# RWKV-6 attention and MLP on one core: the D product is scaled in its PSUM bank, and the order is dealt anew

## The chip, the core and the metric

The kernel runs on one core of one Trainium2 chip. Its engines run side by side, each through its own queue in order: TensorE (PE: matmuls; PEld: its weight loads), VectorE (DVE), ScalarE (ACT), GpSimd (POOL) and SyncE (SP), which issues most DMAs. Matmuls write PSUM, which has eight banks; the other engines read it from there. The metric is device time in microseconds, the median of several runs.

## The reference

A linear attention with a decaying state, then a layer norm and a two-layer MLP with a residual. Batch 4, 8 heads, 768 steps, head size 48, so 384 features; the hidden layer has 1536.

```python
for t in range(S):
    kt, vt, rt, wt = (k[:, :, t], v[:, :, t], r[:, :, t], w[:, :, t])
    cur = np.einsum('bhd,bhe->bhde', u[None] * kt, vt)
    y[:, :, t] = np.einsum('bhd,bhde->bhe', rt, state + cur)
    state = wt[:, :, :, None] * state + np.einsum('bhd,bhe->bhde', kt, vt)
x = np.ascontiguousarray(attn_out.transpose(0, 2, 1, 3)).reshape(B, S, H * D)
mu = np.mean(x, axis=-1, keepdims=True)
var = np.mean((x - mu) ** 2, axis=-1, keepdims=True)
xn = (x - mu) / np.sqrt(var + 1e-06) * g_ln
ch = np.maximum(xn @ w_ch1, 0.0) @ w_ch2
return (x + ch).astype(np.float32)
```

## The kernel before

**Rounds.** The work is cut into eight rounds: four batches, two halves of 384 steps each. A round's `front` does the attention. It transposes `w`, `k` and `r` on TensorE (`w_ps`, `k_ps`, `r_ps`) and builds the products of steps within blocks of 64 in six levels. `quads` issues a level's matmuls (output `a`, 48 rows deep, packed four at a time into quarters of the array), `grow` multiplies `k` and `r` by decay products on VectorE before the next level, and `keep` collects the results. Then come `states` (tiled matmuls of `k` and `v`), and `outputs` (more tiled matmuls into `a`). The matmuls of these three use quarters of TensorE's array and are called tiled here; all others use the whole array. `back` normalizes and runs the MLP.

**The MLP in three parts.** For rounds 1 to 7 (`THREE = 1`) the first product is not done in full fp32. The input is split into a high part H, a low part L and a difference D = L - H/4096; the weights into a high part, the rest times 4096, and the difference of these two. With E12 = 1/4096, the product is (1 + E12)(L product + H product) + D product, with each part in the format fp32r. For a chunk `f` of 128 hidden features (twelve to a round, 84 in all) `mlp` plans:

- `stream`: SyncE fetches the D weights, `d`.
- `go_d` (L1466): three matmuls of D into a bank `hd_ps`. The trace has one record for each.
- `copy` (L1474): ScalarE copies that bank to `h` in SBUF, which frees the bank.
- `go` (L1479): three matmuls of L (`wl`) and three of H (`wh`) into a second bank `h_ps`.
- `add` (L1491): VectorE makes `h = (1 + E12) * h_ps + h`.
- rounds 1 to 4: `relu` (L1497) on ScalarE, in place in SBUF, then the second product in plain fp32 (`o`, three groups of output rows, four times three hidden chunks each; two records a matmul).
- rounds 5 to 7 (`LAST = NR - 3`): `thirds` (L1332). ScalarE makes the relu'd high part H (`high`), VectorE a low part (`low`) and a difference (`diff`), and nine matmuls bring a chunk into the output, D into one bank, L and H into another. After the last chunk VectorE adds the D bank to `x` (`add`), then (1 + E12) times the other (`rest`), and SyncE stores.

Round 0 does the first product in plain fp32 (`first_product`, `h_ps<-xf,w`).

**What sets the order.** No order is written out. Each step is given to `plan.add` with an engine, a cost, what it reads and writes, and a priority; `Plan.order` deals all of them out, engine by engine, simulating the time by those costs. `SHIFTS` (L90) moves priorities, `WAIT` says how much later an engine may start a step of better priority, `STAY` what a change between tiled and whole-array matmuls counts for TensorE, `PATIENCE` how long GpSimd may hold off beside VectorE. A step marked `EITHER` goes to VectorE or GpSimd, whichever the plan finds free. Where TensorE would stand idle in the first 90 us, the plan puts fillers (`idle`), matmuls on zeros.

**Buffers.** `HOMES` gives each kind of tile its number of places: twelve for `h`. PSUM has two double banks `a` for the tiled work (in rounds 5 to 7 they hold two of the three output row groups) and four banks `b` for everything else; the third output row group takes two of the four in rounds 5 to 7 (`o_2P`, `o_2D`). A place comes free when the plan has seen its last reader.

Helper `InOrder` issues every instruction, so nearly all rows of the profile carry its line, L50, and are told apart by the names of their tiles.

```python
plan.add("ACT", 0.45, copy, r=[ps_d], w=[h_], pri=EVICT)
plan.add("DVE", 0.53, add, r=[ps], w=[h_], pri=EVICT)
```

Of the kernel before, what the change touches and what calls it, by code (L numbers as in the profile page):

```python
# [10 lines left out]
F32 = mybir.dt.float32  # L11
# [5 lines left out]
AF = mybir.ActivationFunctionType  # L17
ALU = mybir.AluOpType
# [48 lines left out]
class Plan:  # L67
# [11 lines left out]

    HOP, MARGIN, FILLED, PATIENCE, STAY = 0.1, 0.05, 60.0, 15.1983, 20.0356
    BEFORE, PIECE, FETCH, CROWD = 66, 256, 3.72835, 300
    WAITS = 1.006
    DRAIN = {True: 0.1, False: 0.12}
    WAIT = {"PE": 0.0403625, "ACT": 0.191784, "DVE": 0.109619, "POOL": 0.0526016, "SP": 0.0742572}

    SHIFTS = {  # L90
        -280: 9, -217: 13, -40: 14, -19: 28, -6: 19.5, 0: 8, 1: -20.5, 5: -18, 6: -131.5, 11:
        -21, 16: -8, 18: -18.5, 38: -9.5, 42: 5, 48: -51.5, 52: -22.5, 58: -28, 61: -5, 64: -42,
        67: -35, 88: 4.5, 98: -23, 120: -1, 130: -51, 131: 13, 136: -3, 162: 3.5, 170: -9, 172:
        -17, 174: 11, 182: 43, 184: -6, 204: 2, 205: 9, 206: 40.5, 209: 2, 212: -3, 247: 46,
        262: -4.5, 289: 34, 301: 0.5, 319: -15, 407: 3.5, 411: 9.5, 413: 11, 415: -8, 417: 57,
        423: 52, 441: 13, 448: 6, 451: 114.5, 452: -3.5, 453: 12, 455: 15, 465: -2.5, 480: -32,
        489: 49, 493: 18.5, 499: 9, 502: 10.5,
    }

    def __init__(self, homes, dynamic):  # L100
# [176 lines left out]
def kernel(  # L277
# [147 lines left out]
    def at(rnd, stage):  # L425
        return 40 * rnd + stage
# [661 lines left out]
    def x_parts(rnd, kc):  # L1088
        return [
            tile_(tag, name, [P, 1 if tag == "rest" else 2, RN], F32R)[:, i]  # L1090
            for tag, name, i in x_places(rnd, kc)
        ]
# [238 lines left out]

    def thirds(rnd, f):  # L1332

        x_, h_, (g, c) = f"x{rnd}", f"h{rnd}_{f}", divmod(f, KC + 1)
        b, f0 = rounds[rnd]
        H_, L_, D_ = (f"h{n}{rnd}_{f}" for n in "HLD")
        pri = at(rnd, FILL) + 2 * f + 3
# [1 line left out]
        def out_tiles(i):  # L1339
            if i < 2:  # L1340
                t = tile_("a", f"o{rnd}_{i}", None)
                return t[:, 0, 0:RN], t[:, 1, 0:RN]
            return [tile_("b", f"o{rnd}_{i}{n}", [P, RN]) for n in "PD"]
# [15 lines left out]
                in1=tiles[L_].bitcast(F32), op0=ALU.mult, op1=ALU.add,  # L1359
            )  # L1360

        plan.add("ACT", 0.53, high, r=[h_], w=[H_], new=[("h", H_)], pri=at(rnd, 30))
        plan.add("DVE", 0.56, low, r=[h_, H_], w=[L_], new=[("h", L_)], pri=at(rnd, 30), port=True)
        plan.add("DVE", 0.5, diff, r=[H_, L_], w=[D_], new=[("h", D_)], pri=at(rnd, 30), port=True)
        first, last = f == 0, f == FC - 1
        whole = x_of(rnd)
        for i in range(TT):
            o = f"o{rnd}_{i}"
            names = [o] if i < 2 else [o + "P", o + "D"]

            def go_d(i=i):
                PE.matmul(
                    out_tiles(i)[1], tiles[D_][:, ts(i, P)], tiles[f"w2d{f}"], start=first, stop=last
                )

            def go(i=i):
                to = out_tiles(i)[0]
                PE.matmul(
                    to, tiles[L_][:, ts(i, P)], tiles[f"w2l{g}"][:, c], start=first, stop=False
                )  # L1380
                PE.matmul(
                    to, tiles[H_][:, ts(i, P)], tiles[f"w2h{g}"][:, c], start=False, stop=last
                )

            def both(i=i):
                go_d(i)
                go(i)

            def add(i=i):
                x = tiles[x_][:, i]  # L1390
                DVE.tensor_tensor(
                    out=x, in0=out_tiles(i)[1].rearrange("p (h d) -> p h d", d=D), in1=x, op=ALU.add
                )

            def rest(i=i):
                x = tiles[x_][:, i]
                DVE.scalar_tensor_tensor(
                    out=x, in0=out_tiles(i)[0].rearrange("p (h d) -> p h d", d=D),
                    scalar=1.0 + E12, in1=x, op0=ALU.mult, op1=ALU.add,
                )  # L1400

            def store(i=i):
                SP.dma_start(
                    out=out[b, ds(f0 * RN + i * P, P), :].rearrange("t (h d) -> t h d", d=D),
                    in_=tiles[x_][:, i],
                )

            keys = [o + n if i == 2 else (o, n) for n in "PD"]
            need = [H_, L_, D_, f"w2d{f}", (f"w2h{g}", c), (f"w2l{g}", c)]
            if first:  # L1410
                need += x_of(NR - 1)
            if last and rnd == NR - 1:

                plan.add("PE", 0.18, go_d, count=2, r=need, w=keys[1:], pri=pri - 100, lat=0.17)
                plan.add("PE", 0.36, go, count=4, r=need, w=keys[:1], pri=pri, lat=0.17)
            else:
                plan.add(
                    "PE", 0.525, both, count=6, r=need, w=keys,
                    new=[("a" if i < 2 else "b", n) for n in names] if first else [],
                    pri=pri, lat=0.17,  # L1420
                )
            if last:
                plan.add("DVE", 0.53, add, r=[keys[1]] + whole, w=[(x_, "sum", i)], pri=EVICT)
                plan.add("DVE", 0.53, rest, r=[keys[0], (x_, "sum", i)], w=[(x_, "out", i)], pri=EVICT)
                plan.add("SP", 0.36, store, r=[(x_, "out", i)], pri=EVICT, lat=2.0, size=0.65)
# [27 lines left out]
    def mlp(rnd):  # L1453
# [3 lines left out]
        for f in range(FC):  # L1457
            pri = at(rnd, FILL) + 2 * f * (rnd >= LAST)
            h_, ps, g, cols = f"h{rnd}_{f}", f"h_ps{rnd}_{f}", f // G, ts(f % G, P)
            tag = "h" if rnd < LAST + (f < KC) else ("rk", "vo", "vo")[f % 3]  # L1460
            if rnd < THREE:
                continue
            ps_d, d_ = f"hd_ps{rnd}_{f}", f"d{rnd}_{f}"
            stream(rnd, f)

            def go_d(ps_d=ps_d, d_=d_):  # L1466
                t = tile_("b", ps_d, [P, RN])
                for kc in range(KC):
                    PE.matmul(
                        t, tiles[d_][:, kc], x_parts(rnd, kc)[2],  # L1470
                        start=kc == 0, stop=kc == KC - 1,
                    )

            def copy(h_=h_, ps_d=ps_d, tag=tag):  # L1474
                if tag != "h":
                    tiles[h_] = homes.tile([P, NH * ROW], F32, tag=f"{tag}{plan.place[h_]}", name=h_)[:, 0:RN]
                ACT.copy(out=tile_(tag, h_, [P, RN]), in_=tiles[ps_d])

            def go(ps=ps, g=g, cols=cols):  # L1479
                t = tile_("b", ps, [P, RN])  # L1480
                for kc in range(KC):
                    PE.matmul(
                        t, tiles[f"wl{g}"][:, kc, cols], x_parts(rnd, kc)[1], start=kc == 0, stop=False
                    )
                for kc in range(KC):
                    PE.matmul(
                        t, tiles[f"wh{g}"][:, kc, cols], x_parts(rnd, kc)[0],
                        start=False, stop=kc == KC - 1,
                    )

            def add(h_=h_, ps=ps):  # L1491
                DVE.scalar_tensor_tensor(
                    out=tiles[h_], in0=tiles[ps], scalar=1.0 + E12, in1=tiles[h_],
                    op0=ALU.mult, op1=ALU.add,
                )

            def relu(h_=h_):  # L1497
                ACT.activation(out=tiles[h_], in_=tiles[h_], func=AF.Relu)

            plan.add(  # L1500
                "PE", 0.53, go_d, count=6, r=[d_] + [x_keys(rnd, kc)[2] for kc in range(KC)], w=[ps_d, ps_d + "t"],
                new=[("b", ps_d), (tag, h_)], pri=pri,
                lat=0.17,
            )
            plan.add("ACT", 0.45, copy, r=[ps_d], w=[h_], pri=EVICT)
            plan.add(
                "PE", 1.11 if rnd < LAST else 1.05, go, count=12,
                r=[(f"wl{g}", kc) for kc in range(KC)] + [(f"wh{g}", kc) for kc in range(KC)]
                + [key for kc in range(KC) for key in x_keys(rnd, kc)[:2]]
                + [ps_d if rnd < LAST else ps_d + "t"],  # L1510
                w=[ps], new=[("b", ps)], pri=pri - 0.1, lat=0.17,
            )
            plan.add("DVE", 0.53, add, r=[ps], w=[h_], pri=EVICT)
            if rnd >= LAST:
                thirds(rnd, f)
                continue
            plan.add("ACT", 0.53, relu, w=[h_], pri=at(rnd, 30))
        if rnd >= LAST:
            return
        for i in range(TT):  # L1520
# [178 lines left out]
```

## Time and profile before

| | |
|---|---|
| runs | 526.66, 522.78, 523.22 us; median 523.22 |
| profiled execution, first to last instruction | 521.6 us |
| between it and the median of the runs | 1.6 us |
| first and last matmul | 0.99 us, 517.5 us |
| granted TensorE clock | 0.999 on average |
| bytes moved | 55.84 MB, mean 107 GB/s |

How to read it: the page gives for each engine its busy time, share of the span and number of instructions. A group of instructions is written out<-in with its shapes, the number of instructions, then busy us, mean ns of one, then the idle time of the engine just before them and what ended it. A timeline row is: start in us, time in us, engine, line, operation, out<-in, shapes, number of instructions, and in brackets the idle time before it and what ended that. Matmuls overlap, so the time of a row is longer than the step to the next row's start; a "duration" of 338 ns goes with a start every 176. `issue` means that the engine waited for nothing that the profile shows.

### The profile page before, as it was taken

Reading aid. Unit: us, or ns where it says so; the run is one execution under the profiler, and the core shown is the slowest. Engines: PE = TensorE matmul, PEld = TensorE weight load, DVE = VectorE, ACT = ScalarE, POOL = GpSimd, SP = SyncE. Lnnn points to the kernel's source line nnn. Section 1 sums busy time; section 2 is a strip of 40 time slices with the busy share of each in tenths; the row PEclk is TensorE's granted clock in tenths of the full one; section 3 lists DMA queues with packets and bytes.
Section 4 is the critical chain, followed back from the end, with each engine's and each line's share of the span. In section 5 each row is a group of like instructions: output and inputs, shape, how many; then the busy total and the mean of one; then the engine's idle time right before and its main releaser. Section 6 shows DMA issues by size and latency. Waiting matters only on the chain.

```text
span 521.6 us, 20645 instructions
## 1 busy us (share of the span) xinstructions
PE 514.1 (99%) x8998; PEld 434.4 (83%) x8998; DVE 397.5 (76%) x844; ACT 270.8 (52%) x603; POOL 72.2 (14%) x106
## 2 busy tenths in 40 slices
PE   9999999999999999999999999999999999999996
PEld 6788888767998777989866897589767999999996
DVE  5888999889999898998985773168757867665555
ACT  3798888874375362664630984027373534332321
POOL 7212301221141031122200220003000000000000
PEclk9999999999999999999999999999999999999999
DMA  9966885278635716756420415022012422222201
GB/s 216 257 173 164 192 219 153 76 176 208 164 63 111 179 30 124 163 105 121 126 52 18 98 55 140 17 87 58 1 33 65 134 62 90 77 61 91 77 0 47
DMA packets 122362, 55.84 MB, mean 107 GB/s; under 512 B 93984, under 2 KB 119200, under 8 KB 122272
## 3 DMA queue, kind: packets, MB, share of 16 engines
q1 hardware_dynamic: 119152, 53.54, 40.9%
q10 hardware_dynamic: 3120, 0.98, 1.0%
q8 instruction: 71, 1.16, 0.9%
q14 instruction: 19, 0.16, 0.1%
HBM read 45.05 MB, written 7.10 MB: 100 GB/s over the span
## 4 chain that ended last, share of the span: by engine, by line
PE 97%; DVE 1%; ACT 1%; issue 1%; DVEq 0%
PE a L50 26%; PE o L50 22%; PE h_ps L50 22%; PE hd_ps L50 9%; PE w_ps L50 3%; PE k_ps L50 3%; PE r_ps L50 3%; PE idle L50 3%; PE o_2P L50 2%; PE kn_ps L50 2%; PE xT_ps L50 1%; PE o_2D L50 1%; DVE xhl L50 0%; DVE x L50 0%; DVE xd L50 0%
## 5 line engine op out<-in xcount | busy, mean ns | idle before, releaser
L50 PE MATMUL o<-ffn,h 128*128 128x384 f32 x360 | 124.9, 491 | 0.0
L50 PEld LDWEIGHTS o<-ffn,h 128*128 128x128 f32 x360 | 65.5, 190 | 37.1
L50 ACT COPY h<-hd_ps 128x384 f32<-128x384 f32 x84 | 40.3, 481 | 72.6 <-PE hd_ps L50 70.9
L50 DVE SCALAR_TENSOR_TENSOR h<-h_ps,h 128x384 f32<-128x384 f32 x84 | 46.7, 556 | 39.9 <-PE h_ps L50 37.8
L50 PEld LDWEIGHTS a<-r,k 48*63 48x63 f32 (+5 forms) x4608 | 63.4, 126 | 15.9 <-issue 6.6
L50 PE MATMUL a<-r,k 48*63 48x32 f32 (+5 forms) x4608 | 69.6, 212 | 1.0 <-issue 0.9
L50 PE MATMUL h_ps<-xhl,wl 128*128 128x384 f32 x252 | 59.8, 345 | 0.0
L50 PE MATMUL h_ps<-xhl,wh 128*128 128x384 f32 x252 | 57.7, 337 | 0.0
L50 PE MATMUL hd_ps<-xd,d 128*128 128x384 f32 x252 | 55.5, 346 | 0.1
L50 DVE TENSOR_TENSOR k<-k,tot 112x768 f32<-112x768 f32 (+1 forms) x50 | 40.2, 805 | 18.8 <-PE a L50 18.5
L50 PEld LDWEIGHTS hd_ps<-xd,d 128*128 128x128 f32 x252 | 44.1, 188 | 2.0 <-issue 0.7
L50 PEld LDWEIGHTS h_ps<-xhl,wh 128*128 128x128 f32 x252 | 45.2, 188 | 0.0
L50 PEld LDWEIGHTS h_ps<-xhl,wl 128*128 128x128 f32 x252 | 44.2, 188 | 1.1
L50 DVE COPY_PREDICATED A<-mask,a 128x768 f32<-128x768 int8 (+2 forms) x36 | 39.5, 1097 | 1.1 <-PE a L50 1.1
L50 DVE TENSOR_TENSOR r<-r,tot 112x768 f32<-112x768 f32 (+1 forms) x50 | 39.6, 791 | 0.0
L50 ACT ACTIVATE hH<-h 128x384 fp32r<-128x384 f32 x36 | 18.5, 524 | 37.9 <-DVE h L50 30.0
L50 ACT ACTIVATE h<-h 128x384 f32<-128x384 f32 x48 | 25.2, 526 | 20.8 <-DVE h L50 20.6
L50 ACT COPY A<-a 32x384 f32<-32x384 f32 (+2 forms) x36 | 15.6, 433 | 36.5 <-PE a L50 36.1
L50 DVE SCALAR_TENSOR_TENSOR hL<-h,hH 128x384 fp32r<-128x384 f32 x36 | 20.0, 555 | 10.8 <-ACT hH L50 10.5
L50 POOL TENSOR_TENSOR rk<-nat,nat 128x576 f32<-128x576 f32 (+1 forms) x13 | 17.8, 1368 | 74.9 <-PE a L50 19.7
L50 PE MATMUL h_ps<-xf,w 128*128 128x128 f32 (+1 forms) x144 | 26.3, 332 | 0.0
L50 ACT COPY r<-r_ps 112x384 f32<-112x384 f32 (+1 forms) x31 | 14.2, 493 | 23.2 <-PE r_ps L50 23.1
(119 smaller groups left out, 1007.7 us busy)
## 6 DMA issues: line engine op xcount, KB each, us to landing
d<-w1d SPq DMA_DIRECT2D x84, 192.0 KB, 2.9
raw<-in_moe_w_ch_dram SPq DMA_DIRECT2D x24, 384.0 KB, 4.3
v<-in_v_dram SPq DMA_DIRECT2D x48, 96.0 KB, 3.3
out_dram<-x SPq DMA_DIRECT2D x24, 192.0 KB, 2.0
nat<-in_w_dram SPq DMA_DIRECT2D x36, 96.0 KB, 3.4
nat<-in_k_dram SPq DMA_DIRECT2D x36, 96.0 KB, 3.1
nat<-in_r_dram SPq DMA_DIRECT2D x36, 96.0 KB, 3.2
w1d<-w1diff SPq DMA_DIRECT2D x12, 192.0 KB, 4.0
```

Source lines behind the costliest of these rows:

```text
L50: ins = self.tc.keep_in_program_order(f(*args, **kw))
```

## The change

The D product stays in its bank. ScalarE multiplies the bank in place by 1/(1 + E12) (`shrink`), and the L and H matmuls accumulate on it instead of starting a bank of their own. The bank then holds the first product divided by (1 + E12). VectorE's `add` and the SBUF copy are gone. In rounds 1 to 4 the relu reads the bank, multiplies by (1 + E12) and writes `h`. In rounds 5 to 7 `high` and `low` read the bank itself, without the factor, so the final `add` and `rest` of `thirds` carry one factor of (1 + E12) more. The place for `h` (or for H, L and D) is taken when the D product starts.

The constants of the plan and all of `SHIFTS` are replaced, so the whole order of all engines differs, and so does what `EITHER` gives to GpSimd: its products fall from 70 to 44. The matmuls are the same in kind and number, but for the fillers.

```diff
-    HOP, MARGIN, FILLED, PATIENCE, STAY = 0.1, 0.05, 60.0, 15.1983, 20.0356
+    HOP, MARGIN, FILLED, PATIENCE, STAY = 0.1, 0.05, 60.0, 36.9760452, 44.9511633
-    WAIT = {"PE": 0.0403625, "ACT": 0.191784, "DVE": 0.109619, "POOL": 0.0526016, "SP": 0.0742572}
+    WAIT = {"PE": 0, "ACT": 0.1862803, "DVE": 0.1548472, "POOL": 0.157666, "SP": 0.7767392}
     SHIFTS = {
-        -280: 9, -217: 13, -40: 14, -19: 28, -6: 19.5, 0: 8, 1: -20.5, 5: -18, 6: -131.5, 11:
+        -472: 60.5, -360: -211.5, -38: -20.5, -32: -113.5, -31: -113.5, -29: -113.5, -22: -111.5,
...
     def thirds(rnd, f):
-        x_, h_, (g, c) = f"x{rnd}", f"h{rnd}_{f}", divmod(f, KC + 1)
+        x_, h_, (g, c) = f"x{rnd}", f"h_ps{rnd}_{f}", divmod(f, KC + 1)
...
             def add(i=i):
-                DVE.tensor_tensor(
-                    out=x, in0=out_tiles(i)[1].rearrange("p (h d) -> p h d", d=D), in1=x, op=ALU.add
+                DVE.scalar_tensor_tensor(
+                    out=x, in0=out_tiles(i)[1].rearrange("p (h d) -> p h d", d=D),
+                    scalar=1.0 + E12, in1=x, op0=ALU.mult, op1=ALU.add,
                 )
...
             def rest(i=i):
...
-                    scalar=1.0 + E12, in1=x, op0=ALU.mult, op1=ALU.add,
+                    scalar=(1.0 + E12) ** 2, in1=x, op0=ALU.mult, op1=ALU.add,
...
-            def go_d(ps_d=ps_d, d_=d_):
-                t = tile_("b", ps_d, [P, RN])
+            def go_d(ps=ps, d_=d_):
+                t = tile_("b", ps, [P, RN])
...
-            def copy(h_=h_, ps_d=ps_d, tag=tag):
...
-                ACT.copy(out=tile_(tag, h_, [P, RN]), in_=tiles[ps_d])
+            def shrink(ps=ps):
+                ACT.activation(out=tiles[ps], in_=tiles[ps], func=AF.Copy, scale=1 / (1 + E12))
...
             def go(ps=ps, g=g, cols=cols):
-                t = tile_("b", ps, [P, RN])
-                    PE.matmul(
-                        t, tiles[f"wl{g}"][:, kc, cols], x_parts(rnd, kc)[1], start=kc == 0, stop=False
-                    )
...
+                for n, nm in ((1, "l"), (0, "h")):
+                    for kc in range(KC):
+                        PE.matmul(
+                            tiles[ps], tiles[f"w{nm}{g}"][:, kc, cols], x_parts(rnd, kc)[n],
+                            start=False, stop=(n, kc) == (0, KC - 1), skip_group_check=True,
+                        )
-            def add(h_=h_, ps=ps):
-                DVE.scalar_tensor_tensor(
-                    out=tiles[h_], in0=tiles[ps], scalar=1.0 + E12, in1=tiles[h_],
-                    op0=ALU.mult, op1=ALU.add,
-                )
-            def relu(h_=h_):
-                ACT.activation(out=tiles[h_], in_=tiles[h_], func=AF.Relu)
+            def relu(h_=h_, ps=ps):
+                ACT.activation(
+                    out=tile_("h", h_, [P, RN]), in_=tiles[ps], func=AF.Relu, scale=1 + E12
+                )
```

The three `plan.add` of the chunk (D matmuls, `shrink`, L and H matmuls) write the same bank, one after another; before, the D bank and the L and H bank were two tiles; the plan put L and H after D, but they waited for no ScalarE.

## The prediction

> **What bounds the kernel now.** I read the page's first part, its slices and its chain of waits, then the busy time by stretch, then TensorE's timeline, then the groups that the change touches.
>
> ```profile
> span 521.6 us, 20645 instructions
> PE 514.1 (99%) x8998; PEld 434.4 (83%) x8998; DVE 397.5 (76%) x844; ACT 270.8 (52%) x603; POOL 72.2 (14%) x106
> ...
> PE 97%; DVE 1%; ACT 1%; issue 1%; DVEq 0%
> ```
>
> The chain is TensorE's own queue for 97% of its length. Where time could still be lost is read from the stretches (us from the start; length; busy time of each engine, TensorE first):
>
> ```profile
> 0.00:60.00 60.00, 57.06 (x1291) 46.81 (x1292) 48.18 (x131) 44.97 (x104) 20.70 (x53) 1.00 0.82 198
> 60.00:130.00 70.00, 69.92 (x1324) 54.37 (x1323) 64.37 (x130) 52.60 (x123) 10.53 (x12) 1.00 0.68 170
> 130.00:380.00 250.00, 249.57 (x5372) 204.14 (x5371) 193.43 (x393) 120.98 (x269) 39.92 (x41) 1.00 0.38 90
> 400.00:521.00 121.00, 117.53 (x755) 115.36 (x753) 77.47 (x152) 40.64 (x84) 1.02 (x1) 1.00 0.23 69
> ```
>
> From 60 us on TensorE has no gaps worth the name (0.08 of 70 us, 0.43 of 250), at a granted clock of 1.00. A busy TensorE can still be slow, so I take its starts, one matmul to the next, at the middle of each kind: `o` 323 ns x360, `go` (`h_ps`) 174 x504, `go_d` (`hd_ps`) 176 x252, thirds 175 x324, and so on through all 8998. They make 493.7 us of the 516.5 between first start and last end. The other 22.9 us are all that any new order can touch without removing matmuls. Most of them is this:
>
> ```profile
> 251.31 2.10 PE L50 MATMUL o<-ffn,h 128*128 128x384 f32 x6
> 253.24 0.74 PE L50 MATMUL kn_ps<-ident,k 112*128 112x112 f32 x6
> 253.91 1.56 PE L50 MATMUL a<-r,k 48*62 48x32 f32 x96
> 255.29 0.73 PE L50 MATMUL a<-v,k 64*48 64x48 f32 x48
> ...
> 256.58 2.11 PE L50 MATMUL o<-ffn,h 128*128 128x384 f32 x6
> 258.63 0.76 PE L50 MATMUL a<-v,k 64*48 64x48 f32 x48
> ```
>
> Six `o` take 1.93 us when a whole-array matmul follows (253.24-251.31), 2.05 when a tiled one does (258.63-256.58); over all such rows 1.94 and 2.03. A level of 96 tiled matmuls takes 1.38 when tiled work follows (255.29-253.91) and 1.49 when whole-array work does (five rows). Going into tiled work thus costs 0.09 to 0.12, coming out 0.11. The order has 156 such borders, 78 in each direction: 78 x 0.20 = 15.6 us. What remains is 2.3 us of the first load's landing (the fillers end, nothing is there yet), four holes of 0.28 to 0.69 us inside tiled runs (2.2 us), which the profile puts down to issue, and about 3 us in pieces of a tenth.
>
> **The matmuls.** Same kinds and counts in the changed program: 252 D, 504 L and H, 324 thirds, 360 `o`. Nothing is removed on the bounding engine. Only fillers shrink, from 5760 columns to 5632; 14.6 us/5760 x 128 = -0.3 us.
>
> **Borders.** The instruction order of the changed program has 136, ten pairs fewer: 10 x 0.20 to 0.23, I take -2.1 us.
>
> **What leaves VectorE.**
>
> ```profile
> L50 ACT COPY h<-hd_ps 128x384 f32<-128x384 f32 x84 | 40.3, 481 | 72.6 <-PE hd_ps L50 70.9
> L50 DVE SCALAR_TENSOR_TENSOR h<-h_ps,h 128x384 f32<-128x384 f32 x84 | 46.7, 556 | 39.9 <-PE h_ps L50 37.8
> ```
>
> 84 adds of 556 ns go: -46.7 us. 26 products come over from GpSimd (ten `rk` at 0.75, the rest `tot`, `decay`, `vo`, `w2t` at 0.2 to 0.95): about +14 us. VectorE ends near 365 us. TensorE did not wait for it, so this is worth 0. The cover is 60 to 130 us, where VectorE is busy 64 of 70 us; there are no adds of this kind there (the first D matmul is at 128.9 us), so nothing is gained there. If all of GpSimd's 10.5 us of that stretch came over, at VectorE's half to two thirds of the price, VectorE would have 70 to 71 us of work in 70: a loss of 1 us at most, which I leave in the range.
>
> **ScalarE.** 84 copies become 84 scalings from bank to bank. No row has ScalarE write PSUM. Bounds: the copy's 481 ns below; above, the dearest ScalarE row of that shape that reads PSUM, `xf<-xT_ps` with its scale from memory, 579. I take 491: ACTIVATE out of `h_ps` takes 278 ns for 128 columns and 384 for 256, 0.83 a column, so 491 for 384. The relu of 48 chunks and the H of 36 (526, 524) now read the bank: 491 too. ScalarE is idle half the time; length alone costs 0.
>
> The Trainium skill's ScalarE: Activation LUTs, section What ACT_TABLE_LOAD costs, gives 186 ns + 0.833 a column for an immediate scale, by which an estimate would be 506, not 491; the rows have 172 + 0.83 a column, and the sum would change by 15 ns on a covered step, so by nothing.
>
> **The new wait.** L and H of a chunk wait for ScalarE in the bank, with all of TensorE's queue behind them. The trip begins as before:
>
> ```profile
> 426.20 0.69 PE L50 MATMUL hd_ps<-xd,d 128*128 128x384 f32 x3
> ...
> 426.73 0.34 PE L50 MATMUL a<-w2d,hD 128*128 128x384 f32 x1
> ...
> 426.93 0.48 ACT L50 COPY h<-hd_ps 128x384 f32<-128x384 f32 x1 [2.04 <-PE hd_ps L50]
> ```
>
> ScalarE starts 0.20 us after the slot that follows the last D matmul (426.73 to 426.93). Then 0.49 of scaling, then the way to the weight load. The rows where a load waited for ScalarE show 0.05 to 0.37; the one whose output is the same tile has 0.11. Sum 0.80, bounds 0.73 and 0.20+0.58+0.37 = 1.15. Against it I hold the work that the new order puts between a chunk's D and its L: 0.53 us once, 0.85 to 0.98 four times, 1.05 twenty-four times (two D's, or one chunk's L and H), 1.48 or more fifty-five times. At 0.80 one chunk waits 0.27. At 1.15: 0.62 + 2 x 0.30 + 2 x 0.17 + 24 x 0.10 = 4.0. I take 0.3.
>
> **The next chain.** In rounds 5 to 7, H, L and D' (0.49, 0.556, 0.556) stand between a chunk and its third products: 0.20 + 0.49 + 0.03 + 0.56 + 0.05 + 0.56 + 0.11 = 2.0 us, cover 2.10 for eleven chunks and 2.4 or more for the rest. Cost 0.1, at most 11 x 0.16 = 1.8 if the pick-up takes 0.37. The level chain of tiled work (two VectorE products of 0.95 to 0.97, and hops) needs about 2.3 us; its shortest cover grows from 2.4 to 3.0 us: 0.
>
> **Banks.** A chunk held two banks for 0.53+0.20+0.48 and 1.05+0.27+0.56, 3.1 bank-us. Now it holds one for D, cover, L and H, 0.69 to ScalarE's end and 0.59 more for VectorE's read in the last rounds: 3.9 at a cover of 1.05. There two of four banks belong to `o`; two chunks take 6.3 us of TensorE, so 12.6 bank-us stand against 7.8. Cost 0.
>
> The skill's PSUM — Partial Sum Buffer, section Summary: rules for kernel authors, speaks against this change: empty banks promptly, PSUM is tight. If it decided, the 36 chunks of the last rounds would queue for a bank, by an estimate 36 x (3.9 - 3.1) = 29 us; the rows say they fit.
>
> **The end.** VectorE's last add used to start at 517.51, behind another output's product. The new order finishes that output ten matmuls before the end, so the add waits only for its own D: about -0.3 us. The store after it is the same.
>
> **Sum**: 521.6 - 0.3 - 2.1 + 0.3 + 0.1 - 0.3 = 519.3 of span. The profiled execution lay 1.6 us under the 523.2 median of the runs, so 520.9 us.
>
> **Rivals.** A, slower: the trip through the bank is longer than rows show, because a ScalarE write to PSUM is dear or another ACTIVATE of about 0.5 us stands ahead in ScalarE's queue. 29 chunks have 1.06 us of cover or less, so each tenth over 1.05 costs 2.9 us; from 1.31 the total passes +1%. At 1.4: 29 x 0.35 + 1.2 = 11.4, so 532 us. Against it: in the last rounds the order puts the two scalings ahead of both H's. For it: no row shows the write.
> B, faster: the order also loses the other stalls. 22.9 - 15.6 = 7.3 us, less 2.3 for the landing: 5 us, so 516; half of it is 518.5. For it: VectorE has 32 us less to do. Against it: nothing in the trace shows TensorE late for that reason after 60 us.
> C, slower by a little: longer tiled runs meet the issue holes. Eight runs of 88 to 96 products were there, and eight of 92 to 96 are now; the next size, 72, goes from three to nine. Doubling or tripling four holes of 0.55 costs 2 to 5 us and takes back the borders: 523 to 526.
> D: the first 60 us, where order and loads are dealt anew, are longer or shorter by the 2 to 5 us in which TensorE has gaps there (60 - 57.06): 516 to 526.
>
> **Chances.** Forecast (518.5 to 524): 0.48. A 0.13, B 0.19, C 0.10, D 0.10. The likeliest gives 521. The range 515 to 529 takes in B and D and leaves out most of A. One per cent, which is what a measurement here tells from no change, is 518.0 and 528.5: faster 0.25 (B, half of D, a little of the forecast), slower 0.16 (A and the far end of C and D), same 0.59.
>
> **What would show it.** TensorE's starts should add to the same 493 us, with 136 borders of the same price; a D to L wait appears as idle time of `h_ps` weight loads with ScalarE as releaser, some tenths in all; ScalarE's `h_ps` rows near 490 ns; VectorE near 365 us busy. I am wrong if that releaser shows more than 4 us, if scalings take over 0.6, if there are new holes in tiled runs, or if the first 60 us of work end elsewhere.

## The result and the profile after

The changed kernel took 522.21 us (median of 20 runs, 519.55 to 525.04) beside 524.06 for the kernel before on the same chip (20 runs): ratio 0.9952, 95% interval 0.9931 to 0.9974. Measured again beside the first experiments it took 521.87 against 523.61, ratio 0.9961 (0.9940 to 0.9982). So it is faster by 0.4 to 0.5%, about 2 us. The prediction's sum had 520.9, a gain of 2.3 us.

The page of one execution, first part and chain:

```profile
span 521.5 us, 20493 instructions
...
PE 510.5 (98%) x8994; PEld 431.8 (83%) x8994; DVE 370.5 (71%) x786; ACT 270.4 (52%) x603; POOL 48.9 (9%) x80
...
PE 92%; DVE 5%; DMA 1%; issue 1%; ACT 0%; SPq 0%; DVEq 0%; ACTq 0%
```

This execution was one of the longer ones (523.2 us); its span is only 0.1 us under that of the kernel before, 521.6. The second profiled execution spans 519.3, the number that the prediction's sum gave. Both are read below. The chain is no longer TensorE alone: VectorE has 5% of it (3% in the second profile) and DMA 1%. The stretches show where (start and end in us, length, then PE, PEld, DVE, ACT, POOL busy, clock, DMA share, GB/s):

```profile
0.00:60.00 60.00, 57.96 (x1305) 47.63 (x1306) 50.42 (x136) 43.89 (x104) 19.55 (x48) 1.00 0.83 202
60.00:130.00 70.00, 68.82 (x1310) 53.34 (x1308) 63.70 (x127) 54.62 (x126) 15.50 (x17) 1.00 0.65 163
130.00:380.00 250.00, 247.58 (x5470) 203.47 (x5471) 184.84 (x379) 125.58 (x280) 12.82 (x15) 1.00 0.39 91
400.00:521.00 121.00, 116.13 (x752) 114.48 (x750) 59.35 (x115) 40.67 (x85) 1.02 (x1) 1.00 0.23 71
```

TensorE has 0.9 us less idle time than before in the first 60 us, but 1.2 us of it in the second stretch (0.08 before) and 2.4 in the third (0.43 before). What it waited for, from the list of waits (sum in us, times, longest):

```profile
PEld a L50 <- issue: 10.7, 36, 0.7
...
PE h_ps L50 <- DMA d<-w1d: 1.8, 2, 1.0
PEld h_ps L50 <- issue: 1.8, 2, 1.4
```

The row of `DMA d<-w1d` is new. The timeline shows it at the first two groups of D products of the program:

```profile
127.70 1.90 PE L50 MATMUL h_ps<-xd,d 128*128 128x384 f32 x9 [0.78 <-DMA d<-w1d]
...
130.64 0.76 PE L50 MATMUL h_ps<-xd,d 128*128 128x384 f32 x3 [1.05 <-DMA d<-w1d]
```

The new wait for ScalarE, about which the prediction worried most, is one row of 0.4 us (below). The groups that the change touched:

```profile
L50 ACT ACTIVATE h_ps<-h_ps 128x384 f32<-128x384 f32 x84 | 39.9, 475 | 65.8 <-PE h_ps L50 62.9
L50 ACT ACTIVATE h<-h_ps 128x384 f32<-128x384 f32 x48 | 23.5, 490 | 21.8 <-PE h_ps L50 21.1
L50 ACT ACTIVATE hH<-h_ps 128x384 fp32r<-128x384 f32 x36 | 17.7, 491 | 45.9 <-PE h_ps L50 45.7
```

Scaling from bank to bank takes 475 ns; the same reading written to SBUF takes 490.

### The profile page after: what moved, and what is told of

The parts are those of the page before. It is cut to its first block, busy times and chain, and to the rows that moved or that the text cites. A ratio compares the mean times of both kernels' runs of the same rounds, so it can differ in the third digit from the quotient of the medians.

```text
span 521.5 us, 20493 instructions
## 1 busy us (share of the span) xinstructions
PE 510.5 (98%) x8994; PEld 431.8 (83%) x8994; DVE 370.5 (71%) x786; ACT 270.4 (52%) x603; POOL 48.9 (9%) x80
## 3 DMA queue, kind: packets, MB, share of 16 engines
q8 instruction: 71, 1.16, 0.9%
## 4 chain that ended last, share of the span: by engine, by line
PE 92%; DVE 5%; DMA 1%; issue 1%; ACT 0%; SPq 0%; DVEq 0%; ACTq 0%
PE h_ps L50 30%; PE a L50 25%; PE o L50 22%; PE w_ps L50 3%; PE k_ps L50 2%; PE idle L50 2%; PE o_2P L50 2%; PE r_ps L50 2%; PE kn_ps L50 2%; PE xT_ps L50 1%; PE o_2D L50 1%; DVE x L50 1%; DVE r L50 1%; DMA d<-w1d 1%; DVE k L50 1%
## 5 line engine op out<-in xcount | busy, mean ns | idle before, releaser
L50 PEld LDWEIGHTS a<-r,k 48*48 48x48 f32 (+5 forms) x4608 | 63.2, 126 | 14.1 <-issue 6.9
L50 ACT ACTIVATE h_ps<-h_ps 128x384 f32<-128x384 f32 x84 | 39.9, 475 | 65.8 <-PE h_ps L50 62.9
L50 PE MATMUL a<-r,k 48*48 48x32 f32 (+5 forms) x4608 | 69.4, 212 | 0.9 <-issue 0.8
L50 DVE SCALAR_TENSOR_TENSOR hL<-h_ps,hH 128x384 fp32r<-128x384 f32 x36 | 20.0, 556 | 53.9 <-ACT hH L50 53.7
L50 PE MATMUL h_ps<-xd,d 128*128 128x384 f32 x252 | 54.7, 345 | 2.1 <-DMA d<-w1d 1.8
L50 PEld LDWEIGHTS h_ps<-xd,d 128*128 128x128 f32 x252 | 43.5, 188 | 4.0 <-issue 1.8
L50 ACT ACTIVATE h<-h_ps 128x384 f32<-128x384 f32 (+2 forms) x72 | 31.4, 437 | 26.2 <-PE h_ps L50 25.4
L50 PE MATMUL a<-w2d,hD 128*128 128x384 f32 x72 | 24.4, 342 | 0.0
L50 PEld LDWEIGHTS a<-v,A 64*64 64x64 f32 x384 | 20.6, 133 | 4.4 <-issue 2.1
L50 PE MATMUL a<-w2h,hH 128*128 128x384 f32 x72 | 24.2, 337 | 0.0
```

Of the source, the lines that this page charges most:

```text
L50: ins = self.tc.keep_in_program_order(f(*args, **kw))
```

## The experiments

The ratios are to the kernel before, which ran beside every experiment (523.6 to 524.1 us). The changed kernel ran beside the result and the first four experiments only (522.2 and 521.9 us); "over the changed kernel" means over these.

**again.** The changed kernel unedited.

> The changed kernel itself once more, as the yardstick of the runs beside it, and for a second profile of the same program. If the holes in TensorE's queue (four holes of 0.69 to 1.3 us in tiled runs or just behind them, and 1.8 us of waiting for the D weights at 127 and 130 us) belong to the program, they stand at the same places again; if they are chance, they move. Expected: ratio to before 0.993 to 0.998; the wait for the D weights is there again, 1 to 2.5 us; the holes in tiled runs move, 1 to 4 us in all.

Measured: 521.87 us, ratio 0.9961 (0.9940 to 0.9982), span 519.3. The waits for D's weights were 0.8 us here instead of 1.8. Three holes in TensorE's starts of 0.5 to 1.4 us stand at the same instructions as in the first profile (near 214, 232 and 295 us): they belong to the program, not to the execution. Expected was that the holes move. The ones inside tiled runs kept their places too, but not their lengths: 0.8 and 0.5 us at 31 and 53 us in the first profile, 0.3 and 1.0 in the second.

**noshrink.** The trip through the bank without ScalarE. The scaling of the D product is left out, so L and H follow D at once; order and matmuls stay.

```diff
             def shrink(ps=ps):
-                ACT.activation(out=tiles[ps], in_=tiles[ps], func=AF.Copy, scale=1 / (1 + E12))
+                return
```

> The changed kernel without ScalarE's scaling of the bank (left out: the D product is not divided by 1 + 1/4096); order of everything else the same. TensorE's L and H matmuls then wait for no ScalarE. Theory: the trip through the bank is covered by the order and costs 0.3 to 0.5 us, so this is 0 to 0.6 us faster than the changed kernel (ratio to it 0.999 to 1.000). Rival: the trip costs several us that the profile does not put down to ScalarE: 3 to 5 us faster (0.990 to 0.994).

Measured: 522.48 us (520.61 to 525.46), ratio 0.9977 (0.9957 to 0.9997), span 519.3. Without the trip the kernel is not faster: its cost lies under what can be measured. Tenths could hide, for this profile has 1.9 us of waits for D's weights where again has 0.8.

**twice.** The trip made longer: two scalings one after the other.

```diff
-                ACT.activation(out=tiles[ps], in_=tiles[ps], func=AF.Copy, scale=1 / (1 + E12))
+                for s in (2.0, 0.5 / (1 + E12)):
+                    ACT.activation(out=tiles[ps], in_=tiles[ps], func=AF.Copy, scale=s)
```

> The changed kernel with two scalings of each bank in place of one (by 2, then by half of 1/(1 + 1/4096)); order of everything else the same. The trip from the last D matmul's slot to L's weight load grows from about 0.73 us (0.20 + 0.475 + 0.05) to 1.25. Theory (each tenth over the cover of 1.05 costs 2.9 us, because 24 chunks have that cover and five less): 24 x 0.20 + 0.72 + 2 x 0.40 + 2 x 0.27 = 6.9, less the 0.4 that is lost already: 6 to 7 us slower than the changed kernel, 528 to 529 us. Rival 1: ScalarE is idle half the time and TensorE has other work: under 1.5 us slower. Rival 2: ScalarE's queue carries the delay on into relu and H: over 12 us slower.

Measured: 531.36 us (529.0 to 532.36), ratio 1.0139 (1.0108 to 1.0170): 9.5 us more than the changed kernel. Its list of waits:

```profile
PEld h_ps L50 <- ACT h_ps L50: 10.6, 28, 0.9
PEld a L50 <- issue: 10.1, 35, 0.6
```

The row that was 0.4 us now has 10.6 in 28 waits, about the number of chunks (29) whose cover the prediction had counted at 1.06 us or less. So noshrink does not say that the trip is harmless: it is covered, and one more scaling (0.47 us) is not. The price was a third to a half over the 6 to 7 us expected. The steps between TensorE's starts show why: the first L matmuls come 6.4 us later in all than in again, the sum that was expected, and the second L matmul behind each wait another 0.1 us, 2.6 us in all. Rival A was a real mechanism, below its threshold.

**first_d.** The waits for D's weights. The first four loads are issued by ScalarE's queue, so that they need not stand behind SyncE's other transfers.

```diff
-            SP.dma_start(
+            (ACT if rnd == THREE and f < 4 else SP).dma_start(
```

> The changed kernel, but the first four loads of D weights in round 1 are issued by ScalarE's queue, where they stand between its copies of x, and no longer behind the four swaps of v in SyncE's queue (issued from 124.18 us on). Theory: the 1.8 us that TensorE waits for these loads is lost time on the path, so the kernel is 1.5 to 2 us faster than the changed kernel (ratio to it 0.996 to 0.997). Rival: the next late thing (the x parts, or the loads behind these) takes its place: same as the changed kernel within 0.5 us.

Measured: 526.40 us, ratio 1.0052 (1.0034 to 1.0070), so 4.5 us slower than the changed kernel; what was expected fell. ScalarE's timeline:

```profile
124.97 0.84 ACTq L50 DMA_DIRECT2D d<-w1d  x2
125.86 0.52 ACT L50 ACTIVATE xhl<-xf 128x384 fp32r<-128x384 f32 x1 [2.06 <-DMA vx<-v]
127.03 0.33 ACTq L50 DMA_DIRECT2D d<-w1d  x1
127.40 0.52 ACT L50 ACTIVATE xhl<-xf 128x384 fp32r<-128x384 f32 x1 [1.02 <-DMA d<-w1d]
129.31 0.33 ACTq L50 DMA_DIRECT2D d<-w1d  x1
129.74 0.58 ACT L50 ACTIVATE xf<-xT_ps,g_sb 128x384 f32<-128x384 f32 x1 [1.81 <-DMA nat<-in_w_dram]
```

ScalarE is in order. An issue stays at the head of its queue until what it waits for is there (idle time of 1 to 2 us before the rows that follow an issue), and behind it stand the steps that make the D product's other operand. In the changed kernel the last of these, `xhl<-xf`, begins at 124.47 us; here at 130.35. The loads did not come early either: they took 4.7 to 6.6 us from issue to landing, where the changed kernel's of this stretch took 2.5 to 4.3. The row of waits for D's weights grew to 3.1 us, and the granted clock was 0.91 over 120 to 140 us, where it was 1.00. An issue moved to another engine's queue took its wait with it.

**early_d.** The same aim on SyncE's own queue: the first four loads stand before the four transfers `vx<-v` instead of behind them, 2 to 4 us earlier. The edit takes these four entries of the finished order and puts them before the two `vx` entries; their buffers are free by then.

```diff
+            at = done.index(op)
...
+            vx = [i for i in range(at) if done[i] and done[i].eng == "SP" and any("vx" in n for n in done[i].uses)][-2:]
+            new = max(low + 1, vx[0])
+            if low + 1 <= vx[1]:
+                out.insert(new, out.pop(at)); done.insert(new, done.pop(at))
```

> The changed kernel with the first four loads of D's weights in the first third-width round issued by SyncE ahead of the four transfers vx<-v that stood before them, so some 2.7 us earlier; every other instruction is in its place. Theory (the two waits of TensorE for D's weights, 1.8 us together in one profile of the changed kernel and 0.8 us in the other, are an exposed cost of the new order that only SyncE's queue makes): the row for these waits falls under 0.3 us and the median goes from 521.9 to 520.3 to 521.0. Rival 1 (another stall takes their place, as in the run without ScalarE's scaling, where holes for no visible reason grew instead): 521.9, ratio within 0.002 of the changed kernel's. Rival 2 (the four later vx transfers hold up vo and with it the next tiled products): up to 2 us slower, with a new wait for DMA vx or for vo in the rows of TensorE or VectorE.

Measured: 522.45 us (12 runs), ratio 0.9976 (0.9950 to 1.0001), span 521.4. The row for D's weights is gone, and the time is not shorter. The timeline of its round:

```profile
146.07 0.76 DVE L50 TENSOR_TENSOR rk<-nat,nat 128x576 f32<-128x576 f32 x1 [3.80 <-DMA nat<-in_r_dram]
...
149.94 0.95 DVE L50 TENSOR_TENSOR r<-r,tot 112x768 f32<-112x768 f32 x1
...
150.94 0.25 PE L50 MATMUL a<-r,k 48*32 48x32 f32 x5 [1.78 <-DVE r L50]
```

VectorE, in order, stands before a product of the next round's `r`, whose load landed late, and the last level's `r` waits behind it. TensorE loses 1.8 us there instead. Rival 1 had it: the stall moved. The next limit was 20 us further on.

**late_d.** The same aim from the other side: the plan is told the measured time to landing of a D load.

```diff
-            new=[("rest", name)], pri=EVICT, lat=2.2, size=0.65,
+            new=[("rest", name)], pri=EVICT, lat=3.7, size=0.65,
```

> The changed kernel with the planner told that a load of D's weights takes 3.7 us from issue to landing (measured 3.7) instead of 2.2: the order differs only in the rounds with D, there are 136 borders, and in the first third-width round one rest product now stands ahead of the fourth D product, so that the wait for its weights has work before it; one trip through the bank has only 0.33 us of cover. Theory (the waits for D's weights in the first such round, 0.8 to 1.8 us, shrink by half and nothing else moves): 521.0 to 521.6. Rival (as with the earlier loads, another stall takes their place): 521.9 to 523.

Measured: 523.98 us, ratio 0.9998 (0.9971 to 1.0025), span 521.7: a miss. A D load was still waited for (1.4 us), and the trips through the bank with less cover now show 2.0 us of waits. Its interval overlaps that of the changed kernel, so whether it is slower can't be told.

**struct.** The new product with the plan's constants of the kernel before. No diff is needed: the block of constants and `SHIFTS` is the one that the change removes.

> The new first product (scaling in the bank, relu from the bank), but with the planner's constants of the kernel before; the planner then makes 164 borders between tiled and whole-array work instead of 136, and two of the 84 products stand directly behind their D product with nothing between. Theory (the gain is the borders', not the structure's): 28 borders are 14 pairs at 0.20 to 0.23 us, 2.8 to 3.2 us more, and two uncovered trips at about 1.0 us each add 2: median 526 to 527.5, slower than the kernel before by 2 to 3.5 us. Rival (the structure itself, one VectorE pass and one bank less, gives the gain and the order little): 521 to 523. If the uncovered trips cost nothing, as the run without the scaling suggests for the covered ones, 524.5 to 525.5.

Measured: 537.02 us (536.38 to 538.31), ratio 1.0251 (1.0208 to 1.0294), 10 us past what was expected. Of the 16 us between its span and the shorter one of the changed kernel, 7.5 come before the first third product (413.4 us against 405.8) and 7.8 from there to the last matmul. The waits after 395 us:

```profile
PEld a L50 <- DVE x L50: 2.5, 2, 1.9
PEld h_ps L50 <- ACT h_ps L50: 2.1, 3, 0.9
PEld h_ps L50 <- DVE hL L50: 2.0, 4, 0.6
...
PEld a L50 <- DVE hD L50: 1.9, 2, 1.6
```

In the changed kernel's second profile that stretch has 0.4 us for ScalarE and 0.3 for `hD`. The new product in an order that was not found for it is slower than the old one: the structure alone does not give the gain. The reverse, the old product under the new constants, was not run, so whether the order would gain without the structure stays open.

**new_stay20.** Only the price of a border goes back.

```diff
-    HOP, MARGIN, FILLED, PATIENCE, STAY = 0.1, 0.05, 60.0, 36.9760452, 44.9511633
+    HOP, MARGIN, FILLED, PATIENCE, STAY = 0.1, 0.05, 60.0, 36.9760452, 20.0356
```

> The changed kernel with the planner's price of a border (STAY) as it was before, 20.04 instead of 44.95; it makes 150 borders instead of 136, with the same warming matmuls, and still prices waits for instructions. Theory (borders at 0.20 to 0.23 us a pair): 7 pairs are 1.4 to 1.6 us, median 523.3 to 523.5. If other stalls of a newly dealt order decide: 522 to 529, and then the row of borders is the smaller part of the difference between it and the changed kernel.

Measured: 525.30 us (523.97 to 528.4, 10 runs), ratio 1.0031 (1.0011 to 1.0051): 3.4 us over the changed kernel. Seven border pairs are 1.4 to 1.6 of them; the rest are other stalls of the new order, as the row of `issue` before tiled loads shows (13.5 us against 10.7 and 11.0). By that price the borders are at most half of the difference.

**border and noborder.** The price of a border by itself: in the middle of 42 levels one more matmul of one column stands, over the whole array or over one tile. Its result goes to a column that nobody reads.

```diff
+                 if rnd and uu:
+                     PE.matmul(
+                         tiles[name][:, 0, 500:501], zeros, nought, start=True, stop=True
+                     )
```

> The changed kernel with one more matmul of one column, over the whole array, in the middle of each of 42 levels of tiled products (seven rounds, six levels); its result goes to a column that nobody reads. It is compared with the next run, whose extra matmuls are of one tile and make no border. Theory (a border pair costs the 0.20 to 0.23 us read from the starts of matmuls): 42 pairs are 8.4 to 9.7 us over the next run, median 531 to 533. Rival (the pairs in the profile look dear because the work behind a border is new work that must wait for its operands anyway; the switch itself costs some 0.05 us): 2 to 3 us over the next run, 524.5 to 526.

> The changed kernel with one more matmul of one column and one 64x64 tile at the same 42 places. Both theories: each takes the time of one more small tiled product, 0.02 to 0.06 us, so 0.8 to 2.5 us in all, median 522.5 to 524.5; also the instruction count shifts by 84, so the holes at instruction fetches may fall elsewhere, plus or minus 1 us.

Measured: border 547.56 us, ratio 1.0463 (1.0417 to 1.0509); noborder 536.84, ratio 1.0247 (1.0210 to 1.0284). The difference is 10.7 us, 0.255 a pair, but this is no clean price: the two runs differ in TensorE's holes as well (8.9 us in border, 13.1 in noborder; see below). The levels themselves tell more. One level of border,

```profile
245.84 0.89 PE L50 MATMUL a<-r,k 48*63 48x32 f32 x48
246.66 0.38 PE L50 MATMUL a<-nought 128*128 128x1 f32 x2
246.97 0.89 PE L50 MATMUL a<-r,k 48*63 48x32 f32 x48
```

and of noborder:

```profile
240.42 0.89 PE L50 MATMUL a<-r,k 48*63 48x32 f32 x48
241.13 0.19 PE L50 MATMUL a<-nought 64*64 64x1 f32 x1
```

Half a level takes 0.82 us before whole-array work (246.66 - 245.84) and 0.71 before tiled work (241.13 - 240.42): coming out costs 0.11, as the prediction read. The way back (246.97 - 246.66 = 0.31) holds the going in and two weight loads of the full array, which the run does not tell apart; the 0.09 rests on the rows of the kernel before. The rival of 0.05 a pair falls by the 0.11 alone. From the first start to the last, such a level takes 1.36 us in the changed kernel, 1.46 in noborder and 1.81 in border.

Noborder itself, where 0.8 to 2.5 us were expected, was 15 us over the changed kernel. At their own places the 42 added matmuls cost 5.9 us: 0.10 in most levels, and 0.35 in the seven of 48*32 products (0.83 to 1.18 us), where a 64*64 tile is itself a change of tile size. The list of waits tells where the rest is:

```profile
PEld a L50 <- issue: 18.5, 40, 1.7
...
PE a L50 <- issue: 8.6, 7, 1.6
```

TensorE stands before tiled matmuls and waits for nothing that the profile shows, 8.6 us in seven places, where the changed kernel has 0.8 in two. The page of every run has a row for a queue that no DMA issue of the program uses; for the changed kernel it is

```profile
q8 instruction: 71, 1.16, 0.9%
```

These 71 packets of 16 KB (1.16 MB) are, by their count, TensorE's program: 17,988 matmuls and loads, some 253 a packet. After the first 16 us, noborder has nine places without a releaser where two starts of matmuls are over 0.48 us apart (13.1 us in all; called holes from here on). Set against the packets' starts in the trace, eight of the nine end 2.3 to 2.7 us after a packet began, the other 3.4. Against the packets' ends they are closer still: all nine end 1.2 to 1.5 us after a packet was done, the odd one too, whose packet took 2.0 us. No two packets begin less than 3.5 us apart. That suggested that the 168 added instructions (42 matmuls, two records each, and their loads), by pushing all later ones along the packets, cost the rest.

**phase.** To test this, the program is pushed along by half a packet and left alone otherwise: 128 more instructions at its very start, before the first input lands.

```diff
+        if not shifted:
+            shifted.append(n)
+            n -= 2 * TT
+            for _ in range(34):
+                PE.matmul(
+                    t[0:HP, 500:501], zeros[0:HP, 0:HP], nought[0:HP], start=True, stop=True
+                )
```

> The changed kernel with two of the first six warming matmuls, which run before the first input has landed, replaced by 34 matmuls of one tile and one column; TensorE's program is 128 instructions longer from its very start, half of the 256 that one 16 KB transfer of its instruction queue holds, and nothing else is changed or moved. It is to explain why 42 small tiled matmuls cost 14 us where 1 to 2.5 were expected: in that run, holes of 1.1 to 1.8 us stand in tiled runs, each ending 2.3 to 2.6 us after an instruction transfer began. Theory (it is where the instruction transfers fall in the program that made them): the holes of TensorE over 0.48 us that no operation ends grow from two or three to six or more, and the median is 526 to 534. Rival (the small matmuls themselves, a change of tile size in the middle of a run, cost 0.3 us each): 521.5 to 523, and the holes stay where they are.

Measured: 538.55 us (537.32 to 540.7), ratio 1.0288 (1.0263 to 1.0313), 16.5 us over the changed kernel. The edit was not as clean as meant: the small matmuls ran slowly that early, and the first transposes began at 13.24 us instead of 7.27, so 6.0 us are the start's. The other 10 are these (list of waits, then a run of tiled matmuls in the timeline):

```profile
PE a L50 <- issue: 10.4, 8, 1.7
```

```profile
144.79 2.17 PE L50 MATMUL a<-r,k 48*56 48x32 f32 x142
148.57 0.53 PE L50 MATMUL a<-r,k 48*62 48x32 f32 x21 [1.61 <-issue]
```

In the changed kernel the same run has no hole:

```profile
138.29 2.61 PE L50 MATMUL a<-r,k 48*56 48x32 f32 x178
140.83 1.32 PE L50 MATMUL h_ps<-xd,d 128*128 128x384 f32 x6
```

There are eight holes (12.1 us in all), where the changed kernel has three (2.2 us); all eight end 2.2 to 2.9 us after a packet began and 1.2 to 1.5 after it was done. The theory stands; the rival's holes would have stayed where they were. A change of tile size does cost what the rival says (0.35 us, in noborder's 48*32 levels), but in seven places only.

**nocrowd.** The plan models such waits: TensorE's program in pieces of 256 instructions (PIECE), 3.73 us apart at least (FETCH), and a price for waiting on one (CROWD). Here the price is 0.

```diff
-    BEFORE, PIECE, FETCH, CROWD = 66, 256, 3.72835, 300
+    BEFORE, PIECE, FETCH, CROWD = 66, 256, 3.72835, 0
```

> The changed kernel with the planner's price of a modelled wait for instructions (CROWD) set to 0, so that it orders work without regard to them; it makes 134 borders instead of 136 and the same warming matmuls. Theory (keeping instruction transfers out of dense tiled runs is a part of what the order gives, larger than the borders): one border pair less is -0.2 us, holes of 1 to 2 us come back in at least four places, median 526 to 532. Rival (the borders are what counts in the order): 521.0 to 522.0.

Measured: 540.14 us (539.13 to 543.23), ratio 1.0324 (1.0296 to 1.0352), with a border pair less than the changed kernel. Its list of waits:

```profile
PE a L50 <- issue: 10.8, 9, 2.0
...
PE h_ps L50 <- DMA d<-w1d: 4.0, 2, 3.7
```

Eleven holes make 13.9 us; ten of them end 2.3 to 2.7 us after a packet began. The D weights' wait grew too, and the granted clock stood at a half for 10.2 us (over 134.7 to 138.1 and 220.0 to 226.8), so not all of the 18 us is the packets'. Still, without its price on such waits the plan loses 18 us, with a lower price on a border (new_stay20) 3.4.

No version beat the changed kernel: early_d, noshrink and late_d lie within what can be told from it, the others above.

## Why the prediction was right

The forecast rests on the borders, and their term came as it stood. The rest of the sum came to the right total only because terms of up to 2 us that it had wrong or left out cancelled, and that is luck.

**Matmuls and borders: right, -2.1 us.** The 20 borders fewer have the price that was read from the kernel before: over the changed kernel's starts, 0.093 us going in and 0.11 to 0.13 coming out at the middle. Ten pairs at 0.20 to 0.22 are 2.0 to 2.2 us. The run border shows the price of coming out at its place; going in was only read from rows.

The Trainium skill (TensorEngine Tiling (Array Packing), section Key Properties) says that a change of tiling mode, not of the tile, drains TensorE. The rows agree: 0.82 against 0.71 us for the same half level, by what follows it.

**The trip through the bank: right in kind, its size 0.1 us under or less.** From the slot after the last D matmul to ScalarE's start took mostly 0.20 us (0.375 from that matmul's start, less 0.175 for its slot), in the others 0.26; the scaling 0.475; from there to the weight load 0.05: 0.73 to 0.79, where 0.80 was taken. L's waits for it were 0.4 us in both profiles, 0.3 in the sum, and noshrink finds nothing. The count of covers was right as well: twice shows 28 waits. (By the prediction's own sum rival A passes 1% at a trip of 1.28 us, not 1.31; nothing hangs on it.)

**VectorE's relief worth nothing: nothing speaks against it, but no run tests it alone.** Its work fell from 397.5 to 370.5 us (365 was predicted). In early_d and struct VectorE is waited for where it stands behind a late operand, not where it is busy.

**The end: wrong, 0.5 us.** The last add was to come 0.3 us earlier. From the last matmul's end to the span's end it is 5.3 us in the first profile and 4.3 in the second, after 4.1 before. The last add explains the 0.2 of the second; the other 1.0 us of the first lies behind the last add (3.8 us to the end, 2.9 in the second profile and before), with the store. The last adds in the timeline of the first profile:

```profile
514.89 1.61 DVE L50 SCALAR_TENSOR_TENSOR x<-a,x 128x384 f32<-128x384 f32 x3
...
516.42 0.55 DVE L50 SCALAR_TENSOR_TENSOR x<-o_2D,x 128x384 f32<-128x384 f32 x1
517.07 0.56 DVE L50 SCALAR_TENSOR_TENSOR x<-o_2P,x 128x384 f32<-128x384 f32 x1
```

The other outputs' adds did go ahead, but four of them in a row (the view cuts the first off), and D's add is behind those: it begins at 516.42, 0.92 us after its own matmul (515.50), and the last add at 517.07, 0.88 after the last matmul's end (516.19); before it was 0.64 (518.17 after 517.53). "Waits only for its own D" was the step that failed; VectorE's queue was in front.

**What was left out: D's weights.** The prediction followed banks, ScalarE and VectorE, but not the loads of `d`. The kernel before has no row of waits for them, the changed one 1.8 and 0.8 us in its two profiles; the term stood at nothing without a reason. Three runs moved this wait, and none was faster for it.

**Rival C: the right place, far too small a price, and not in this kernel.** The holes were put down to longer tiled runs and priced at 2 to 5 us. It is not the run's length that decides but where it meets the packets of the program: half a packet's shift makes 10 us of holes, and a plan without regard to them still more. By the profile's releasers the holes sum to 2.2 us in the changed kernel and 2.0 in the kernel before. Taking also those that end 2.2 to 2.9 us after a packet began but are put down to TensorE's own last matmul (the one at 232 us is) or to nothing, it is 3.5 and 3.6 us in the two profiles of the changed kernel and 3.5 before. So the forecast held because the new order has no more of them than the old one, which nothing in the sum had asked.

**Rivals B and D: did not come.** From 60 us on, TensorE's idle time in the two stretches did not vanish but grew, from 0.5 to 3.6 us in the first profile and 2.3 in the second; in the first 60 us it shrank by 0.9 and 0.7.

Sum of what was seen, from the steps between TensorE's starts, each against the middle of its kind in all three profiles (us, changed less before):

| | first profile | second profile | predicted |
|---|---|---|---|
| borders | -2.0 | -2.0 | -2.1 |
| fillers | -0.7 | -1.0 | -0.3 |
| waits for D's weights | +2.1 | +1.1 | 0 |
| other steps over 0.35 us late | +0.3 | -0.1 | +0.4 (ScalarE's trip, next chain) |
| last matmul's end to the span's end | +1.2 | +0.2 | -0.3 |
| smaller differences | -1.0 | -0.5 | 0 |
| span | -0.1 | -2.3 | -2.3 |

The borders are the only term of size that is as predicted. In the second profile D's weights and the end cost 1.3 us that the sum did not have; fillers, smaller differences and waits that did not come give them back. Why the fillers shrank by more than their 128 columns was not tried. (The steps hold a little more than the rows of waits, which count idle time alone; a step of 1.0 us behind a filler of the kernel before, at 52.9 us, is counted with the late steps.)

## What to carry to other kernels

Before removing or adding instructions on a dense TensorE queue, look at what ends the holes that have no releaser: if they end a fixed time after a packet of the instruction queue, any edit upstream can move them all. An experiment that adds instructions then needs a twin with the same number of them, and even so (border and noborder differ by 4 us of holes) its price is to be read at its place, not from the total. A wait put under cover is free only up to its cover: take it away and make it longer, both, before calling it free. A load that is waited for is not hurried by giving it to another in-order queue; see what stands behind it there.

## What the runs showed of the hardware

- TensorE's program arrives in packets of 16 KB (71 for 17,988 matmuls and loads), never less than 3.3 us apart in any run. Tiled matmuls use a packet's worth in some 1.8 us (an estimate: 96 of them with their loads, 192 instructions, take 1.38 us). TensorE then has holes of 1 to 2 us, ending 2.2 to 2.9 us after a packet's start and 1.2 to 1.7 after its end. The packet before the one that ends a hole began 4.8 to 9.6 us earlier in phase, so it is not two packets close together that make a hole; what does was not found. The Trainium skill (Runtime: NRT & Kernel Launch, section Instruction fetch mechanics) has the 16 KiB blocks of 256 instructions and calls the cost of crossing one mostly hidden. The size agrees; the cost does not: 12 to 14 us of holes in phase and nocrowd.
- In five runs the granted clock fell to a half in the middle of the work, for 3.4 us at a time, once for 6.8, during or within 1.5 us of a wait of TensorE of 1.8 us or more (0.91 over 120 to 140 us in first_d and nocrowd, 0.83 over 220 to 240 in nocrowd). Other waits of that length brought no fall (2.1 us at 148.8 in early_d, 1.9 at 230.7 in phase), so the length alone does not decide.
- ScalarE writes a PSUM bank it has read in 475 ns for 128x384, 15 less than the same reading written to SBUF.
